# Moving K and score-operand transposes to the DMA crossbar in a chunk-select attention with a gated MLP

## The chip, the cores and the metric

The kernel runs on one core of a Trainium2 chip. The metric is the time of one execution in microseconds (us), the median of several. The kernel before takes 208.53 us (208.47 to 208.6, three runs). The profile's span, from the first to the last instruction, is 206.9 us, about 1.6 us less than the time.

Engines: PE is the matmul engine (PEld its weight loads), ACT is ScalarE, DVE is VectorE, POOL is GpSimd, SP is SyncE. In the traces each takes its instructions in the order that the compiler's scheduler chose, and stands if the next one is not ready (PE stood 10.9 us for one operand in the changed kernel). In this kernel POOL issues all loads from memory, and SP issues all transposes that go by DMA and all stores.

## The reference

Four batches, eight heads, 768 positions, head size 64. K is cut into 24 chunks of 32 positions; the extremes of each chunk give an upper bound on its scores, and each query keeps its six best chunks.

```python
k_min = np.min(k_chunks, axis=3);  k_max = np.max(k_chunks, axis=3)
ub = np.sum(np.maximum(q * k_min, q * k_max), axis=-1)          # per query and chunk; later chunks masked
top_chunks = np.argsort(ub, axis=-1)[..., -top_k:]              # top_k = 6
scores = np.where(selected & causal, scale * (q @ k.T), -1e9)
x = softmax(scores) @ v                                         # heads side by side: 768 x 512 per batch
h = np.maximum(x @ w_in, 0);  u, v = split(h)
v_s = w_spatial @ normalise(v) + b_spatial
out = (u * v_s) @ w_out
```

## The kernel before

The 32 heads are handled as 16 pairs, "pair 0" to "pair 15". The MLP of one batch runs on PE between the scores of the next batch's pairs. For each pair: load K and q (POOL), transpose K, take the chunk extremes (DVE), bound, select (DVE), transpose the score operand `a` (q together with the selection), scores (PE), exponential (ACT), zero the upper triangle (POOL), multiply by V (PE), normalise (DVE).

```python
def k_transpose(self):
    if self.i < 16:                                   # always: 6 PE transposes into PSUM
        self.kT = kT = ps_ml.tile([P, S], F16, tag="mlp", name="kTp")
        for t in range(NQT):
            nc.tensor.transpose(kT[:, t * P:(t + 1) * P], self.k[:, t], identity)
    else: ...                                         # crossbar path, not used
def k_max(self):                                      # k_min is the same with min and negate
    nc.vector.tensor_reduce(self.kmm[:, 0, :], self.kT.rearrange("d (c ch) -> d c ch", ch=CHUNK), axis=AX.X, op=Alu.max)
def k_operand(self, hi):                              # score weights from the transposed K
    copy(self.kh[hi][d0:d1], self.kT[d0:d1])
def a_transpose(self, hi):
    if self.i >= 8:                                   # crossbar, issued by SP
        if hi == 0:
            nc.sync.dma_start_transpose(out=self.a.rearrange("d t h s -> d (t h) s"),
                                        in_=self.qs.rearrange("p t c d -> p (t c d)"))
        return
    ...                                               # else 6 PE transposes into PSUM, for each of two halves
def a_copy(self, hi):
    if self.i >= 8: return
    copy = nc.vector.tensor_copy if self.i < 2 and hi == 0 else nc.scalar.copy
    copy(self.a[:, :, hi, :], self.tr...)
def triangle(self, hi):                               # from pair 4 on, by POOL, between its loads
    nc.gpsimd.affine_select(out=blk, in_=blk, compare_op=Alu.is_ge, fill=0.0, ...)
def load_w_spatial(j):                                # six loads of 128 rows of 1536 bytes
    nc.gpsimd.dma_start(out=ws_raw[:, j], in_=moe_w_spatial[j * P:(j + 1) * P, :])
```

The softmax here doesn't subtract the row's maximum and nothing guards it: scores larger than these inputs give would overflow.

Of the kernel before, what the change touches and what calls it, by code (L numbers as in the profile page):

```python
# [11 lines left out]
F16 = mybir.dt.float16  # L12
Alu = mybir.AluOpType
Act = mybir.ActivationFunctionType
AX = mybir.AxisListType

P = 128
CHUNK = 32
# [30 lines left out]
def kernel(  # L49
# [11 lines left out]
    nc = tc.nc  # L61
    B, H, S, D = q.shape
    NCH = S // CHUNK
# [14 lines left out]
    sb = ctx.enter_context(tc.tile_pool(name="sb", bufs=2))  # L78
# [78 lines left out]
    class Pair:  # L157
# [6 lines left out]
            self.e = {}  # L164

        def k_transpose(self):
            if self.i < 16:
                self.kT = kT = ps_ml.tile([P, S], F16, tag="mlp", name="kTp")
                for t in range(NQT):
                    nc.tensor.transpose(kT[:, t * P:(t + 1) * P], self.k[:, t], identity)  # L170
            else:
                self.kT = sb.tile([P, S], F16, tag="kT", name="kT", bufs=3)
                nc.sync.dma_start_transpose(out=self.kT.rearrange("d (t s) -> d t s", s=P),
                                            in_=self.k.rearrange("p t h d -> p (t h d)"))

        def k_max(self):
            self.kmm = sb.tile([P, 2, NCH], F16, tag="kmm", name="kmm")
            nc.vector.tensor_reduce(self.kmm[:, 0, :], self.kT.rearrange("d (c ch) -> d c ch", ch=CHUNK),  # L178
                                    axis=AX.X, op=Alu.max)

        def k_min(self):
            nc.vector.tensor_reduce(self.kmm[:, 1, :], self.kT.rearrange("d (c ch) -> d c ch", ch=CHUNK),  # L182
                                    axis=AX.X, op=Alu.min, negate=True)

        def k_bounds(self):
            for hi, (d0, d1) in enumerate(HALF):
# [54 lines left out]
        def a_transpose(self, hi):  # L241
            if hi == 0:
                self.a = sb.tile([P, NQT, 2, P], F16, tag="a", name="a")
            if self.i >= 8:
                if hi == 0:
                    nc.sync.dma_start_transpose(out=self.a.rearrange("d t h s -> d (t h) s"),
                                                in_=self.qs.rearrange("p t c d -> p (t c d)"))
                return
            self.tr = self.trans_tile()
            for t in range(NQT):  # L250
                nc.tensor.transpose(self.tr[:, t * P:(t + 1) * P], self.qs[:, t, 2 * hi:2 * hi + 2, :], identity)  # L251

        def a_copy(self, hi):
            if self.i >= 8:
                return
            copy = nc.vector.tensor_copy if self.i < 2 and hi == 0 else nc.scalar.copy
            copy(self.a[:, :, hi, :], self.tr.rearrange("d (t s) -> d t s", s=P))  # L257


# [252 lines left out]
    p, n = pairs[0:2]  # L512
# [82 lines left out]
```

## Time and profile before

| | before |
|---|---|
| time | 208.53 us |
| PE, ACT, DVE busy | 91%, 76%, 75% of the span |
| K reduction from PSUM, two per pair | 0.95 us each |
| K operand copy from PSUM, two per pair | 0.55 us each |
| 192 KB K load, issue to landing (median) | 8.1 us |

The page of the kernel before, parts 1 to 6, in part. The rows of digits cut the span into 40 slices of 5.2 us; a digit is the busy share in tenths. PEclk is the clock granted to PE. The q1 line is the queue of transposes and stores: packets, MB, share. The group lines give busy us and mean ns of one; the last lines give KB per issue and median us from issue to landing.

```profile
PE 187.8 (91%) x1922; PEld 115.1 (56%) x1922; DVE 154.5 (75%) x454; ACT 158.1 (76%) x326; POOL 80.5 (39%) x100
...
PE   0368999898899999999999999999999999999992
...
PEclk9999999999999999999999999999999999999999
DMA  5999999999999999979998926648782124540356
...
q1 hardware_dynamic: 37856, 14.75, 36.4%
...
PE 69%; ACT 17%; DVE 8%; issue 2%; DMA 2%; POOL 0%; DVEq 0%; ACTq 0%; POOLq 0%
...
L178 DVE TENSOR_REDUCE kmm<-kTp 128x24 f16<-128x768 f16 x16 | 15.2, 948 | 3.7 <-PE kTp L170 2.7
...
L194 DVE COPY kh<-kTp 64x768 f16<-64x768 f16 x30 | 16.5, 549 | 0.5
...
k<-in_k_dram POOLq DMA_DIRECT2D x14, 192.0 KB, 8.1
qs<-in_q_dram POOLq DMA_DIRECT2D x14, 192.0 KB, 7.5
ws_raw<-in_moe_w_spatial_dram POOLq DMA_DIRECT2D x6, 192.0 KB, 6.9
```

From the 12th slice (57 us) on PE stands at 9, and from 90 to 152 us it is busy throughout. The chain of waits is two thirds PE (69% of the span), so PE's work is what counts there. In the first 80 us the DMA row stands at 9: nearly all loads fall into this stretch, and a load there mostly takes 6 to 9 us to land. POOL issues the loads and also makes the triangles, in one order. In the timeline of the kernel before, pair 4's first triangle stands behind eight or so loads:

```profile
49.62 0.55 POOL L363 DMA_DIRECT2D w_out_sb<-in_moe_w_out_dram  x1 [1.14 <-DMA vt<-in_v_dram]
50.84 2.04 POOL L327 DMA_DIRECT2D k<-in_k_dram  x2 [0.67 <-PE sc L266]
52.93 0.86 POOL L278 TENSOR_SCALAR_AFFINE_SELECT e<-e 128x768 f16<-128x768 f16 x1
```

The columns are start, duration, instruction, and in brackets how long POOL stood and for what. POOL already waits 1.14 us for an earlier load to land before it can issue another one.

### The profile page before, as it was taken

The page shows a single profiled execution, that of the slowest core. Times are in us where ns is not written, and L with a number is a line of the kernel's source. Part 1 is how long each engine was busy: PE and PEld are TensorE (multiplying, and loading weights), DVE is VectorE, ACT ScalarE, POOL GpSimd, SP SyncE. Part 2 cuts the span into 40 slices and gives each one's busy share as a digit, 9 for nine tenths or more (in the row PEclk, how much of TensorE's full clock was granted, in tenths as well). Part 3 has the DMA queues.
Part 4 walks back from the last instruction along what each step waited for, and adds up shares of the span by engine and source line. Part 5 has one row for each costly group of instructions (what it writes and reads, how often), then busy time and mean ns, then how long its engine had stood idle before and what let it go on. Part 6 is the DMA issues. An engine that isn't in the chain of part 4 may idle for free.

```text
span 206.9 us, 5068 instructions
## 1 busy us (share of the span) xinstructions
PE 187.8 (91%) x1922; PEld 115.1 (56%) x1922; DVE 154.5 (75%) x454; ACT 158.1 (76%) x326; POOL 80.5 (39%) x100
## 2 busy tenths in 40 slices
PE   0368999898899999999999999999999999999992
PEld 0266776775666665656655656565555454444440
DVE  6467979989799989899797999887647456365520
ACT  4797989899998889785989996669999830666042
POOL 7997659596992463236114111111111110000000
PEclk9999999999999999999999999999999999999999
DMA  5999999999999999979998926648782124540356
GB/s 38 92 118 154 140 178 158 173 177 167 177 162 162 97 119 128 135 130 147 149 278 153 180 62 57 127 88 158 181 166 65 38 29 92 187 152 3 72 128 256
DMA packets 114424, 27.27 MB, mean 132 GB/s; under 512 B 109536, under 2 KB 110816, under 8 KB 114400
## 3 DMA queue, kind: packets, MB, share of 16 engines
q0 software_dynamic: 76544, 12.20, 89.8%
q1 hardware_dynamic: 37856, 14.75, 36.4%
q8 instruction: 15, 0.25, 0.5%
q14 instruction: 9, 0.07, 0.1%
HBM read 24.38 MB, written 6.29 MB: 148 GB/s over the span
## 4 chain that ended last, share of the span: by engine, by line
PE 69%; ACT 17%; DVE 8%; issue 2%; DMA 2%; POOL 0%; DVEq 0%; ACTq 0%; POOLq 0%
PE mlp L388 40%; PE sc L266 12%; ACT e L271 10%; PE acc L289 7%; PE kTp L170 2%; ACT a L257 2%; DVE kmm L178 2%; PE ub L222 2%; DMA k<-in_k_dram 2%; PE trm L251 2%; ACT vraw L398 1%; PE tr L205 1%; DVE vn L412 1%; DVE kmm L182 1%; ACT u L420 1%
## 5 line engine op out<-in xcount | busy, mean ns | idle before, releaser
L271 ACT ACTIVATE e<-sc 128x512 f16<-128x512 f32 x192 | 96.9, 553 | 14.8 <-PE sc L266 13.4
L266 PE MATMUL sc<-a,kh 128*128 128x512 f16 (+3 forms) x256 | 65.5, 308 | 2.1 <-ACT e L271 1.5
L388 PE MATMUL mlp<-w_in_sb,xT 128*128 128x512 f16 x192 | 53.0, 379 | 0.1
L278 POOL TENSOR_SCALAR_AFFINE_SELECT e<-e 128x768 f16<-128x768 f16 x24 | 20.9, 869 | 66.3 <-ACT e L271 66.3
L289 PEld LDWEIGHTS <-e 128*128 128x128 f16 x672 | 31.4, 97 | 17.0 <-DVE x L297 3.8
L388 PE MATMUL mlp<-vn,wsT 128*128 128x512 f16 x144 | 37.3, 379 | 0.0
L289 PE MATMUL acc<-vt,e 128*128 128x65 f16 x672 | 35.3, 193 | 0.7 <-DVE x L297 0.4
L266 PEld LDWEIGHTS <-kh 128*128 128x128 f16 x256 | 22.7, 98 | 13.3 <-issue 0.8
L437 ACT COPY o<-mlp 128x512 f32<-128x512 f32 x24 | 14.1, 586 | 19.5 <-PE mlp L388 19.1
L400 DVE BATCH_NORM_STATS2 stats<-vraw 128x6 f32<-128x512 f32 x24 | 16.6, 693 | 12.9 <-ACT vraw L398 12.5
L388 PE MATMUL mlp<-w_out_sb,gT 128*128 128x512 f16 x96 | 25.1, 379 | 0.0
L388 PEld LDWEIGHTS <-xT 128*128 128x128 f16 x192 | 17.2, 97 | 12.6 <-issue 0.4
L427 DVE SCALAR_TENSOR_TENSOR g<-mlp,b_col,u 128x512 f16<-128x512 f32 x24 | 17.9, 748 | 7.3 <-PE mlp L388 6.2
L232 DVE MAX8 max<-ub 128x8 f32<-128x8 f32 (+4 forms) x160 | 15.6, 165 | 5.1 <-PE ub L222 4.9
L388 PEld LDWEIGHTS <-wsT 128*128 128x128 f16 x144 | 12.9, 98 | 10.4
L178 DVE TENSOR_REDUCE kmm<-kTp 128x24 f16<-128x768 f16 x16 | 15.2, 948 | 3.7 <-PE kTp L170 2.7
L297 DVE TENSOR_TENSOR x<-acc,rec 128x384 f16<-128x384 f32 x32 | 17.6, 551 | 0.4
L336 POOL DMA_DIRECT2D qs<-in_q_dram x14 | 14.6, 1049 | 5.9 <-PE sc L266 5.9
L194 DVE COPY kh<-kTp 64x768 f16<-64x768 f16 x30 | 16.5, 549 | 0.5
L398 ACT ACTIVATE vraw<-mlp 128x512 f32<-128x512 f32 x24 | 14.4, 601 | 3.0 <-PE mlp L388 3.0
L420 ACT ACTIVATE u<-mlp 128x512 f16<-128x512 f32 x24 | 14.3, 598 | 1.7 <-PE mlp L388 1.5
L327 POOL DMA_DIRECT2D k<-in_k_dram x14 | 14.4, 1045 | 2.5 <-PE kTp L170 1.8
(67 smaller groups left out, 230.2 us busy)
## 6 DMA issues: line engine op xcount, KB each, us to landing
out_dram<-o SPq DMA_DIRECT2D x24, 256.0 KB, 2.3
vt<-in_v_dram POOLq DMA_DIRECT2D x8, 384.0 KB, 8.8
k<-in_k_dram POOLq DMA_DIRECT2D x14, 192.0 KB, 8.1
qs<-in_q_dram POOLq DMA_DIRECT2D x14, 192.0 KB, 7.5
ws_raw<-in_moe_w_spatial_dram POOLq DMA_DIRECT2D x6, 192.0 KB, 6.9
w_in_sb<-in_moe_w_in_dram POOLq DMA_DIRECT2D x8, 128.0 KB, 6.9
w_out_sb<-in_moe_w_out_dram POOLq DMA_DIRECT2D x4, 128.0 KB, 7.9
k<-in_k_dram POOLq DMA_DIRECT2D x4, 96.0 KB, 3.4
```

Source lines behind the costliest of these rows:

```text
L178: nc.vector.tensor_reduce(self.kmm[:, 0, :], self.kT.rearrange("d (c ch) -> d c ch", ch=CHUNK), axis=AX.X, op=Alu.max)
L194: copy(self.kh[hi][d0:d1], self.kT[d0:d1])
L266: mm(sc[:, col:col + n], lhsT=self.kh[hi][:, t * P:(t + 1) * P], rhs=self.a[:, q0 // P:(q0 + n) // P, hi, :], start=True, stop=not diag)
L271: nc.scalar.activation(out=self.e[hi][:, g * 512:g * 512 + width], in_=sc[:, 0:width], func=Act.Exp, scale=scale)
L278: nc.gpsimd.affine_select(out=blk, in_=blk, compare_op=Alu.is_ge, fill=0.0, base=0, channel_multiplier=-1, pattern=[[0, NQT], [1, P]])
L289: mm(self.av[:, qi, :], lhsT=self.e[hi][:, c:c + P], rhs=self.v[hi][:, t, 0:D + 1], start=first and n == 0, stop=last and n == len(blocks) ...
L297: nc.vector.tensor_tensor(self.x16[:, :, hi, :], in0=self.av[:, :, 0:D], in1=rec.to_broadcast([P, NQT, D]), op=Alu.mult)
L388: mm(st[group][:, 0:cols], lhsT=lhsT, rhs=rhs, start=(j == 0), stop=(j == n - 1))
L398: nc.scalar.activation(st["vraw"][:, ti, :], h, func=Act.Relu)
L400: nc.vector.bn_stats(stats, st["vraw"][:, ti, :])
L420: nc.scalar.activation(st["u"][:, ti, :], h, func=Act.Relu)
L427: nc.vector.scalar_tensor_tensor(g, in0=vs, scalar=b_col[:, ti:ti + 1], in1=st["u"][:, ti, :], op0=Alu.add, op1=Alu.mult)
```

## The change

The intent is to take transposes from PE, which is full (91% busy), and copies from ACT; to shorten the reductions on DVE by two halvings of the K that now lies in SBUF (that this would be shorter was the author's estimate, which no trace of this case showed); and to give two early copies to DVE.

```diff
         def k_transpose(self):
-            if self.i < 16:
+            if self.i < 6:
                 ... PE transposes
             else:                       # crossbar, issued by SP
+        def k_bound(self, m, op):       # used by k_max and k_min
+            src = self.kT.rearrange("d (c ch) -> d c ch", ch=CHUNK)
+            if self.i >= 6:
+                for n in (16, 8):
+                    half = sb.tile([P, NCH, n], F16, tag=f"half{n}", name=f"half{n}")
+                    nc.vector.tensor_tensor(half, in0=src[:, :, 0:n], in1=src[:, :, n:2 * n], op=op)
+                    src = half
+            nc.vector.tensor_reduce(self.kmm[:, m, :], src, axis=AX.X, op=op, negate=(m == 1))
         def a_transpose(self, hi):
-            if self.i >= 8:
+            if self.i >= 6:             # crossbar
         def a_copy(self, hi):
-            if self.i >= 8:
+            if self.i >= 6:
                 return
-            copy = nc.vector.tensor_copy if self.i < 2 and hi == 0 else nc.scalar.copy
+            copy = nc.vector.tensor_copy if self.i < 4 and hi == 0 else nc.scalar.copy
```

More of the change, by code (lines that the diff above doesn't have):

```diff
@@ L177, in k_max @@
             self.kmm = sb.tile([P, 2, NCH], F16, tag="kmm", name="kmm")
-            nc.vector.tensor_reduce(self.kmm[:, 0, :], self.kT.rearrange("d (c ch) -> d c ch", ch=CHUNK),
-                                    axis=AX.X, op=Alu.max)
+            self.k_bound(0, Alu.max)
+        def k_bound(self, m, op):
[6 more added lines that the diff above has]
+            nc.vector.tensor_reduce(self.kmm[:, m, :], src, axis=AX.X, op=op, negate=(m == 1))
         def k_min(self):
-            nc.vector.tensor_reduce(self.kmm[:, 1, :], self.kT.rearrange("d (c ch) -> d c ch", ch=CHUNK),
-                                    axis=AX.X, op=Alu.min, negate=True)
+            self.k_bound(1, Alu.min)
         def k_bounds(self):
```

## The prediction

> **What bounds the kernel now.** The page gives PE 91%, ACT 76%, DVE 75% of 206.9 us. In the table of stretches PE is busy throughout from 90 to 152 us, and the chain of waits there is almost only MLP matmuls, two per 0.43 us: PE-bound. From 20 to 75 us the chain runs through ACT (exponentials, score-operand copies L257) and DVE (28.9 to 36.5 us): from 30 to 45 us PE is busy 13.6, DVE 14.4, ACT 14.0 us. The page's DMA row stays at 9 up to about 78 us: the loads' queue is saturated, and a 192 KB load takes 8 us to land.
>
> **What changes, costed.**
> - PE loses 84 transposes (60 of K, 24 of score operands). Six take 0.35 us in the chain, so 4.9 us, 3.2 us of it after pair 6's first score (66 us).
> - ACT loses six copies of 0.80 us (pairs 6, 7: between 59.6 and 74.6 us; pairs 2, 3: early). DVE takes two at 0.55 us.
> - DVE: a reduction from PSUM takes 0.95 us. [...] DVE rarely limits there: worth little.
> - DMA gains ten K and two score-operand transposes, about 2.7 MB in 256-byte packets, several in the saturated stretch.
>
> **The catch: order on SP.** In the instruction order of the changed kernel, SP issues the K transposes of pairs 6 to 10 first and only then pair 6's score operand. Pair 10's K transpose waits for its K load, whose second half POOL issues behind pair 4's first triangle (52.9 us). In the trace what is issued at 53.7 us lands at 62.8; with the new traffic I expect 63 to 66 us. So pair 6's operand is issued at 64 to 68 us, though it is selected at 58.7. A transpose under this load took 8.8 us to land (issued 60.9, first packet 65.0), 6.9 and 8.4 us. [...] It lands at 70 to 76 us, while PE, in order, wants it at about 66. PE and ACT then stand 4 to 9 us. From pair 6's start to the end the old kernel takes 140.5 us; I take off 3.2 us of PE and about 0.7 us of ACT relief. A start at 72 us gives a span of about 208.6, and time is 1.6 us more.
>
> **Prediction: 210.5 us**, 8 in 10 between 205.5 and 214.5. Faster by over 2%: 0.17; within 2%: 0.53; slower by over 2%: 0.30.
>
> **What would show it.** PE idle before the first score matmul of pair 6, ended by the DMA of its operand, 4 us or more; pair 10's K transpose issued after 62 us, right before it. [...] PE-bound pairs 0.35 us shorter.
>
> **What would make it wrong.** The K load of pair 10 landing early, or transposes landing within 5 us: 204 us. DMA contention also delaying spatial weights or the operands of pairs 7 to 9: more than 214 us.

The sum reads: pair 6 starts at 72 us, and 140.5 us from there to the end, less 3.2 us of PE and 0.7 us of ACT, make a span of 208.6 us; 1.6 us more is a time of 210.2 us, put as 210.5. The saving on DVE, "worth little", is not in it.

## The result, and the profile after

The changed kernel took 229.87 us (229.12 to 231.76, four runs), against 208.56 us for the kernel before on the same chip. The ratio is 1.103, with a 95% interval from 1.098 to 1.108: 10% slower. Ratios here are the mean time of one kernel's fast runs over that of the other's of the same rounds, so not quite the ratio of the medians that are quoted.

The same lines of the page of the changed kernel, whose slices are 5.7 us:

```profile
PE 187.8 (83%) x1838; PEld 111.5 (49%) x1838; DVE 152.9 (67%) x496; ACT 155.3 (68%) x320; POOL 80.9 (36%) x100
...
PE   0478998865397029999999799999999999999993
...
PEclk9999999999589857999999999999999999999999
DMA  6999999999999993998999999656759042551247
...
q1 hardware_dynamic: 48992, 17.51, 43.5%
...
PE 45%; DMA 28%; DVE 13%; ACT 8%; issue 3%; POOL 2%; DVEq 0%; ACTq 0%; POOLq 0%; SPq 0%
...
k<-in_k_dram POOLq DMA_DIRECT2D x14, 192.0 KB, 10.5
qs<-in_q_dram POOLq DMA_DIRECT2D x14, 192.0 KB, 8.5
ws_raw<-in_moe_w_spatial_dram POOLq DMA_DIRECT2D x6, 192.0 KB, 11.4
```

Three things are to be seen. PE has two holes (it is idle from 54.5 to 60.6 and from 72.7 to 83.6 us), and the granted clock falls at each (to 0.50 from 58 to 64 us and from 79 to 88 us). The chain of waits is 28% DMA where it was 2%. And a weight load takes 11.4 us to land instead of 6.9.

The DVE groups that the change made, from the view of groups with shapes kept apart (columns as in the group lines above):

```profile
L201 DVE COPY kh<-kT 64x768 f16<-64x768 f16 x20 | 10.3, 516 | 0.3
L185 DVE TENSOR_TENSOR half<-kT 128x384 f16<-128x384 f16 x20 | 7.7, 396 | 3.8 <-DMA kT<-k 3.8
L187 DVE TENSOR_REDUCE kmm<-half 128x24 f16<-128x192 f16 x20 | 6.7, 340 | 0.1
L185 DVE TENSOR_TENSOR half<-half 128x192 f16<-128x192 f16 x20 | 4.8, 242 | 0.0
```

The three steps of one extreme take 0.396 + 0.242 + 0.340 = 0.98 us, no less than the 0.95 us of the one reduction before, and a K operand copy 0.52 us instead of 0.55.

Where the time went is read from the start of each pair's first exponential in the two traces:

| point | before, us | after, us | later by |
|---|---|---|---|
| pair 4, last exponential ends | 54.2 | 61.5 | 7.3 |
| pair 6 starts | 66.6 | 84.3 | 17.7 |
| pair 7 starts | 77.8 | 97.6 | 19.8 |
| pair 10 starts | 107.1 | 128.3 | 21.2 |
| pair 15 starts | 158.2 | 179.1 | 20.9 |
| end of the span | 206.9 | 227.6 | 20.7 |

So the whole loss is there by pair 10, in two large steps, and after it almost nothing is won back. The largest waits of the changed kernel between 44 and 62 us, from the view of waits (engine and line, what ended the wait, us in total, times, longest):

```profile
ACT e L278 <- PE sc L273: 7.2, 2, 5.6
PEld L296 <- POOL e L285: 6.2, 1, 6.2
PE acc L296 <- POOL e L285: 6.1, 1, 6.1
```

The same view between 62 and 90 us:

```profile
ACT e L278 <- PE sc L273: 13.4, 5, 11.0
PEld L273 <- DMA a<-qs: 11.4, 1, 11.4
PE sc L273 <- DMA a<-qs: 10.9, 1, 10.9
```

The first stall: PE stands 6.1 us for POOL's triangle of pair 4. POOL's timeline of the changed kernel shows why:

```profile
52.78 0.56 POOL L367 DMA_DIRECT2D ws_raw<-in_moe_w_spatial_dram  x1 [1.81 <-DMA ws_raw<-in_moe_w_spatial_dram]
55.93 0.54 POOL L370 DMA_DIRECT2D w_out_sb<-in_moe_w_out_dram  x1 [2.60 <-DMA vt<-in_v_dram]
56.99 1.02 POOL L334 DMA_DIRECT2D k<-in_k_dram  x1 [0.52 <-DMA k<-in_k_dram]
58.19 1.42 POOL L350 DMA_DIRECT2D vt<-in_v_dram  x1 [0.18 <-issue]
59.67 0.86 POOL L285 TENSOR_SCALAR_AFFINE_SELECT e<-e 128x768 f16<-128x768 f16 x1
```

The triangle comes at 59.67 us instead of 52.93. Before three of these four loads POOL stands for an earlier load to land, and the earlier loads are late. The second stall is the one that the prediction named, the operand of pair 6. What leads to it, in the timelines of POOL and SP of the changed kernel:

```profile
60.49 1.02 POOL L334 DMA_DIRECT2D k<-in_k_dram  x1
71.90 1.21 SPq L173 DMA_TRANSPOSE kT<-k  x1
73.29 4.31 SPq L253 DMA_TRANSPOSE a<-qs  x1
```

The second half of pair 10's K load is issued behind the late triangle, at 60.49, and lands at 71.76. Pair 10's K transpose waits for it and is issued at 71.90, and only then, at 73.29, the transpose of pair 6's operand, which lands 10.3 us later, at 83.60. The operand was ready for it earlier, but not as early as before: this is its selection on DVE, in the kernel before and in the changed one.

```profile
58.33 0.39 DVE L237 TENSOR_TENSOR qs<-ub,max 128x240 f16<-128x240 f32 x1
66.77 0.39 DVE L244 TENSOR_TENSOR qs<-ub,max 128x240 f16<-128x240 f32 x1
```

So of the 17.7 us at pair 6, the first 8.4 are a later selection, after the first stall (in it DVE waited 5.8 us for PE). From the end of the selection to the start of pair 6 it then took 17.1 us (6.1 until SP issued the operand, 10.3 until it landed, 0.7 until the first exponential) where the kernel before took 7.9. The order on SP can account for 6.1 us at most.

### The profile page after: what moved, and what is told of

Read it like the earlier page. It is cut to its first block, busy times and chain, and to the rows that moved or that the text cites. A ratio compares the mean times of both kernels' runs of the same rounds, so it can differ in the third digit from the quotient of the medians.

```text
span 227.6 us, 4968 instructions
## 1 busy us (share of the span) xinstructions
PE 187.8 (83%) x1838; PEld 111.5 (49%) x1838; DVE 152.9 (67%) x496; ACT 155.3 (68%) x320; POOL 80.9 (36%) x100
## 4 chain that ended last, share of the span: by engine, by line
PE 45%; DMA 28%; DVE 13%; ACT 8%; issue 3%; POOL 2%; DVEq 0%; ACTq 0%; POOLq 0%; SPq 0%
PE mlp L395 29%; DMA qs<-in_q_dram 12%; PE sc L273 7%; DMA kT<-k 5%; ACT e L278 5%; PE acc L296 5%; DMA a<-qs 5%; DMA ws_raw<-in_moe_w_spatial_dram 5%; DVE kmm L187 2%; DVE vn L419 2%; DVE x L304 2%; DVE half L185 2%; DMA k<-in_k_dram 1%; DVE max L239 1%; PE trm L258 1%
## 5 line engine op out<-in xcount | busy, mean ns | idle before, releaser
L273 PE MATMUL sc<-a,kh 128*128 128x512 f16 (+3 forms) x256 | 67.6, 314 | 13.6 <-DMA a<-qs 12.3
L395 PE MATMUL mlp<-w_in_sb,xT 128*128 128x512 f16 x192 | 55.2, 389 | 0.5 <-DMA xT<-x 0.5
L285 POOL TENSOR_SCALAR_AFFINE_SELECT e<-e 128x768 f16<-128x768 f16 x24 | 21.1, 878 | 65.5 <-ACT e L278 65.4
L273 PEld LDWEIGHTS <-kh 128*128 128x128 f16 x256 | 23.0, 99 | 26.4 <-DMA a<-qs 13.3
L395 PEld LDWEIGHTS <-xT 128*128 128x128 f16 x192 | 17.7, 100 | 13.5 <-DMA xT<-x 0.9
L350 POOL DMA_DIRECT2D vt<-in_v_dram x8 | 11.5, 1438 | 25.3 <-PE sc L273 23.6
L395 PEld LDWEIGHTS <-wsT 128*128 128x128 f16 x144 | 13.0, 97 | 10.9
L343 POOL DMA_DIRECT2D qs<-in_q_dram x14 | 14.6, 1046 | 1.3 <-DMA ws_raw<-in_moe_w_spatial_dram 1.1
L419 DVE TENSOR_SCALAR vn<-vraw,mv,rstd 128x512 f16<-128x512 f32 x24 | 12.8, 582 | 1.6 <-ACT rstd L417 1.6
## 6 DMA issues: line engine op xcount, KB each, us to landing
ws_raw<-in_moe_w_spatial_dram POOLq DMA_DIRECT2D x6, 192.0 KB, 11.4
w_out_sb<-in_moe_w_out_dram POOLq DMA_DIRECT2D x4, 128.0 KB, 10.3
```

The lines of the kernel that those rows point to most:

```text
L273: mm(sc[:, col:col + n], lhsT=self.kh[hi][:, t * P:(t + 1) * P], rhs=self.a[:, q0 // P:(q0 + n) // P, hi, :], start=True, stop=not diag)
L343: nc.gpsimd.dma_start(out=t.rearrange("p x t d -> p (x t) d"), in_=source(q, b, h, 2))
L395: mm(st[group][:, 0:cols], lhsT=lhsT, rhs=rhs, start=(j == 0), stop=(j == n - 1))
L419: nc.vector.tensor_scalar(st["vn"][:, ti, :], in0=st["vraw"][:, ti, :], scalar1=st["mv"][:, ti, 0:1], scalar2=st["rstd"][:, ti, :], op0=Al ...
```

## The experiments

18 kernels were run, all with correct results. Each was timed against the kernel before on the same chip. Waits quoted in the text are from the view of waits, landing times from the trace's DMA issues. A run counts as slow here when it is over 1.5% above the fastest of the same kernel. Medians are over all runs. Slow were three of the four runs in program order, and one of four each in the second run of the last pairs (219.61 us), in its partner without halvings (215.25) and in the run with the triangle moved (220.41).

### Two spare transposes, nothing else

The first K transposes that SP issues are those of pairs 6 and 7, at 38 and 39 us. Do they cost anything apart from who waits for them?

```diff
+                if self.i in (6, 7):       # into a tile that nobody reads; K still goes through PE
+                    nc.sync.dma_start_transpose(out=spare..., in_=self.k...)
```

> The kernel before, plus two crossbar transposes of the K of pairs 6 and 7 on SP into tiles that nobody reads (as early as in the changed kernel); every other engine keeps its order, instruction for instruction. Theory A (crossbar transposes starve the loads in the saturated stretch): loads issued from 38 to 46 us land after 12 to 14 us instead of 7 to 8, POOL stalls on its loads and reaches pair 4's first triangle some 6 us late, and the time rises by 4 to 7 us, to 212.5 to 215.5. Theory B (only the order on SP costs time, since an operand waits behind a K transpose): nothing waits for these two, so under 1 us, 208 to 209.5.

Measured: 216.91 us, ratio 1.039 (1.035 to 1.043). The orders on PE, DVE, ACT and POOL are those of the kernel before, so two transposes whose result nobody reads cost 8.2 us. The waits show the first stall of the changed kernel again:

```profile
PEld L293 <- POOL e L282: 7.5, 1, 7.5
PE acc L293 <- POOL e L282: 7.3, 1, 7.3
```

The two transposes took 11.5 and 14.0 us to land, and the loads issued from 38 to 46 us took 11 to 15.6 us (6.1 to 8.4 before). That is Theory A, though the time is above its range (212.5 to 215.5). Issuing took long too: in the changed kernel the second of these two transposes, issued 1.4 us behind the first, held SP for 4.2 us, its other K transposes for 1.2 to 1.9 us.

### The same bytes, not transposed

```diff
-                    nc.sync.dma_start_transpose(out=spare..., in_=self.k...)
+                    nc.sync.dma_start(out=spare[:, :, 0:P], in_=...)    # the same 2 x 192 KB in 256-byte pieces
```

> As dummy67, but the two transfers are plain copies of the same bytes in the same number of 256-byte pieces, from SP. If it is the transposing that starves the loads (A1), the loads keep landing in about 8 us and the time stays within 1 us of before. If any transfer of 768 small packets beside the loads does it (A2), the time is that of dummy67, about 213 to 215 us.

Measured: 210.4 us, ratio 1.009 (1.005 to 1.013), outside both ranges but much nearer to A1. So 6.5 of the 8.2 us are not the bytes but the transposing. The table of stretches, for 41 to 46 us, shows what the DMA engines moved. A line has the stretch, the busy us of PE, PEld, DVE, ACT and POOL with counts, the granted clock, the DMA share, and GB/s as its last number. The kernel before:

```profile
41.00:46.00 5.00, 4.68 (x78) 3.80 (x75) 4.47 (x10) 4.93 (x12) 4.66 (x5) 1.00 1.48 180
```

With the plain copies:

```profile
41.00:46.00 5.00, 4.68 (x79) 3.80 (x77) 4.46 (x10) 4.92 (x12) 4.49 (x5) 1.00 1.27 213
```

With the spare transposes:

```profile
41.00:46.00 5.00, 4.68 (x79) 3.80 (x76) 4.47 (x10) 4.92 (x12) 4.42 (x5) 1.00 1.35 97
```

The rate rises from 180 to 213 GB/s with plain copies and falls to 97 with transposes, all traffic counted. In the trace's DMA records from 38 to 52 us, a 1536-byte packet of the weight load lasts 141 ns on average before and beside the copies, and 298 ns beside the transposes, with single packets up to 2.7 us. The 2048-byte packets of the input weight, some of which ran beside the same transposes, did not lengthen (208 ns, 219 before). And a transpose is not slow everywhere: the fastest 192 KB transpose of the changed kernel, at 105.5 us, landed after 2.8 us, where the two spare ones beside the weight loads took 11.5 and 14.0 us and the plain copies 9 to 10 us.

### Spare transposes later

> The kernel before plus two spare crossbar transposes, now of K of pairs 12 and 13, issued at about 71 us instead of 38 us; nothing reads their result and the other engines' orders are unchanged. Theory A, a transpose is costly only in the stretch from 38 to 52 us where the weight loads with their 1536- and 1024-byte packets are in flight and POOL's triangles stand behind them: 208.0 to 209.7 us, no new wait over 1 us in the largest waits. Theory B, a transpose is costly beside any loads in the saturated stretch: 212 to 217 us as with the transposes of pairs 6 and 7.

Measured: 209.88 us, ratio 1.005 (1.003 to 1.007). Two spare transposes at 71 us cost 1.1 us, just above Theory A's range. The stretch is still full of loads, but of loads in 128-byte packets, and their mean packet duration from 72 to 84 us did not rise (48 ns, before 50). The operand of pair 8, issued some 5 us behind them, landed at 88.8 instead of 86.3 us, and PE waited 1.6 us for it, a wait that the kernel before does not have.

That beside loads in 128-byte packets a transpose cost little more than its bytes is seen in the packet counts too. From 63 to 67 us the changed kernel's trace has some 370 to 470 load packets and 340 to 430 transpose packets each us, and 1170 to 1210 load packets alone in the two us after. So the loads had about a third of their rate while a transpose ran, but the bytes of both together (150 GB/s, then 152) stayed the same. In the kernel before there are 519 load packets (60 of 1024 bytes) and 520 of a transpose from 65.5 to 67.25 us. Beside the spatial weight's load, from 41 to 46 us in the changed kernel, it was otherwise: 101 GB/s in all (180 in the kernel before), and single packets of both kinds lasted up to 2.6 or 2.7 us. What makes them last so long is not shown.

### The order on SP

The rival to the theory of slowed loads was that the order on SP is the loss. Here SP was kept in program order.

> The changed kernel with SP's transfers kept in the program's own order, so that pair 6's score operand is issued right after the K transposes of pairs 6 and 7 and not after that of pair 10. PE's order is the same but for four matmuls. Theory B (SP's order is the whole loss): 206 to 210 us. Theory A+B (starved loads cost the 6 us before 61 us and the later delays, the order costs the 11 us before pair 6): the stall before pair 6 shrinks from 11 us to under 3, that of pair 4 stays near 6 us, and the time is 216 to 221 us.

Measured: 244.77 us, 240.12 to 247.13; three of the four runs, the profiled one among them, are slow, so there is no ratio, but even the fast one (240.12) is far above both ranges. Pair 6's operand was issued at 69.9 instead of 73.3 us, directly after its selection, but DVE now stood 18.9 us in seven waits for K transposes. The size is not to be relied on. It gives no support to the idea that SP's order alone made the loss; since it moved other transfers too, it does not measure what that order costs either.

### Only the score operands of pairs 6 and 7

> The changed kernel with all K transposes back on PE (and so whole reductions from PSUM): what is left is the score operands of pairs 6 and 7 by the crossbar and two copies moved to DVE. Both theories: no K transpose stands before an operand, no transpose runs before 58 us, so no large stall: 206 to 210 us. If the operands of pairs 6 and 7 by themselves land late (issued at 59 us, landing after 68 us), pair 6 starts up to 3 us late and it is 209 to 212 us.

Measured: 218.77 us, ratio 1.046 (1.042 to 1.050). Both theories expected at most 212 us: a miss. K stays on PE; the two early DVE copies are in this run too, 0.6 us by the next one. Pair 6's operand (384 KB, twice a K transpose) was issued at 59.6 us, as soon as it was selected and with nothing ahead of it on SP, and landed only at 71.9, 12.3 us later. Pair 6 starts at 72.7 instead of 66.6. The operand transposes without any K transpose are a loss in this stretch: on PE and ACT they took about 0.35 + 0.8 us per half.

### Only the DVE copies

> The kernel before with only the last part of the change: VectorE copies the first score operand half of pairs 2 and 3. Theory A, VectorE and ScalarE share the early stretch evenly and this part is worth nothing by itself: 208.0 to 209.2 us. Theory B, it takes two 0.8 us copies from a ScalarE that is on the chain of waits: 206.5 to 207.9 us.

Measured: 209.4 us, ratio 1.003 (1.001 to 1.004). The last part of the change, with the order that the scheduler chose for it, is a loss of 0.6 us by itself, just above Theory A's range.

### The change without the early operands

> The changed kernel with the score operands of pairs 6 and 7 back on PE and ScalarE; K of the pairs from 6 on still goes by the crossbar. Theory A, two separate losses: the stall in pair 4 behind the slowed loads stays (POOL before PE, 5 to 7 us), the wait of pair 6 for its operand is gone, and pairs 10 and on still wait for K behind late loads: 217 to 224 us. Theory B, nearly all of the loss is pair 6's late operand: 209 to 213 us. Theory C, the losses overlap and one slow stretch of DMA sets all: 227 to 231 us.

Measured: 225.65 us, ratio 1.080 (1.078 to 1.083). This lies just above Theory A's range. Pair 6 no longer waits for its operand, which had cost some 10 us, but only 4.2 us are won. Pair 6 starts at 75.4, still 8.8 us later than in the kernel before. The stall of pair 4 stays (PE behind POOL, 5.2 us), and in pair 10 a new one comes up: DVE waits for K transposes 9.0 us in three waits, the longest 5.8, and PE and ACT stand behind it. The stalls are not a sum. Removing one uncovers another.

### K by the crossbar for the last pairs only

From pair 12 on the loads are nearly done (the kernel before issues its last one at 110.7 us) and PE is the bound (busy all of the 12 us from 126 to 138 us), so this is where the change should win.

```diff
-            if self.i < 6:
+            if self.i < 12:                                      # halvings from pair 12 on too; a from pair 8, copies as before
+                with tc.issue_after(pairs[self.i - 2].issued.ins):   # K transpose behind the operand of pair i-2
                     nc.sync.dma_start_transpose(kT...)
```

> The kernel before with the crossbar K path and the halvings for pairs 12 to 15 alone, each K transpose issued behind the operand transpose of the pair two earlier. The profile of before has PE as the bound there, and 24 PE transposes at about 0.058 us would be saved, 1.4 us. Theory A, PE's time is what counts there and the crossbar has room: 206.3 to 207.7 us. Theory B, the later K bounds or slower loads of the late pairs eat the gain: 208.2 to 211 us.

Measured: 217.06 us, ratio 1.040 (1.038 to 1.041), outside both ranges, a clear miss. Pair 12's K transpose was issued at 103.3 and landed at 107.5 us; DVE had come to the first halving about 4 us earlier and stood for it, up to 4.4 us in one wait, and DVE's next work (the selection of pair 11, the normalising of pair 9) stood behind it. So the next run issued the transposes earlier, behind the operand of pair i-4.

> K of pairs 12 to 15 by the crossbar as in the run that took 217.06 us, but each K transpose is issued behind the operand transpose of the pair four earlier instead of two, so that it should land at about 88, 93, 107 and 116 us, before VectorE comes to the halvings of that pair (105 us and later in the kernel before). Theory A, the 8.3 us were VectorE standing in order behind a K transpose that had not landed: 206.5 to 209.5 us, no wait of the halvings on a transpose over 1 us. Theory B, halvings or transposes cost by themselves in this stretch: 212 to 218 us.

Measured: 217.41 us, ratio 1.035 (1.031 to 1.040), inside Theory B's range, but its trace shows a wait and not a cost of the halvings by themselves. The scheduler, seeing the transposes earlier, also moved the halvings forward: the first one of pair 12 came to its turn before pair 10's reductions and stood until the transpose landed at 86.8 us. In the view of waits:

```profile
DVE half L186 <- DMA kT<-k: 5.3, 2, 3.0
```

The next run is this one with a place given to the halvings in DVE's order, near where the reductions stood before.

```diff
+                    with tc.issue_after(pairs[self.i - 2].selected.ins):
                         nc.vector.tensor_tensor(half, ...)
```

> Pairs 12 to 15 by the crossbar again, K transposes behind the operand transpose of the pair four earlier, and now also the halvings put behind the selection of the pair two earlier in VectorE's order, near the place of the reductions in the kernel before, so that the K transposes have landed for several us when VectorE comes to them. Theory A, the loss of 8.7 us was the halvings' early place in VectorE's order, where they stand for a transpose: 207 to 210 us and no wait of a halving on a transpose. Theory B, the added transposes cost by themselves here: 212 us or more.

Measured: 210.59 us, ratio 1.007 (1.004 to 1.009). This is 0.6 us above Theory A's range. No wait of a halving on a transpose is left, and 6.8 us are gone by the medians, 5.9 by the ratios. This is the direct test: most of the loss here came from DVE standing in order for a transpose that had not landed. What remains is 1.6 us over the kernel before. PE was spared 24 transposes, 1.4 us, and the kernel still did not become faster.

### Without the halvings

> The same as the run before, with one reduction of the transposed K from SBUF in place of the two halvings and a reduction. In the changed kernel the three steps took 0.34, 0.24 and 0.34 us, together no less than the 0.95 us of the reduction from PSUM. If a reduction from SBUF takes about 0.85 to 0.95 us, halving gains nothing and this run is within 1 us of its partner; if it takes 0.7 us or less, halving was a loss by itself.

Measured: 212.07 us, ratio 1.014 (1.010 to 1.017), 5.3 us better than its partner with halvings (4.5 by the ratios). One reduction from SBUF takes 0.936 us, nearly what it took from PSUM (0.947). The three steps took 0.347 + 0.241 + 0.340 = 0.93 us there. So halving wins nothing on DVE, and the expectation "within 1 us of its partner" failed, it seems because the order changed too: the reductions stand in DVE's order where transposes have landed (one wait of 0.6 us). (The 0.34 us that the expectation gives for the first step is not the changed kernel's; there it took 0.396.)

> The changed kernel with the halvings undone: one reduction of the transposed K from SBUF for each extreme. A reduction from SBUF took 0.936 us in pairs 12 to 15, against 0.98 for the three steps in the changed kernel. Theory A, the stalls come from the transposes alone: 228 to 232 us. Theory B, the halvings add loss by their early place in VectorE's order, as in pairs 12 to 15, where leaving them out took 5.3 us off: 221 to 227 us.

Measured, the same in the changed kernel: 228.37 us, ratio 1.092 (1.089 to 1.095), 1.5 us off 229.87, so Theory A. Ten pairs of halvings are not what makes the large stalls.

### Are wide packets the partner of the transposes?

The weight rows come in packets of 1536 bytes, the K, q and V loads in packets of 128 bytes. The rows of the spatial weight, and in the first pair of runs those of the input weight too, were loaded in 256-byte pieces into padded tiles.

```diff
-    ws_raw = cp.tile([P, NQT, S], F16)
+    ws_raw = cp.tile([P, NQT, NQT, P + 8], F16)
-        nc.gpsimd.dma_start(out=ws_raw[:, j], in_=moe_w_spatial[j * P:(j + 1) * P, :])
+        nc.gpsimd.dma_start(out=ws_raw[:, j, :, 0:P], in_=moe_w_spatial[...].rearrange("p (c e) -> p c e", e=P))
```

> A control for the next run: the kernel before with the rows of two weights (1536 and 2048 bytes) loaded in 256-byte pieces into padded tiles; nothing goes by a new transpose. The bytes are the same, the order of a few instructions moves. 207.5 to 212 us; its own time matters only as the base of the next run.

> The run before this one plus the two spare crossbar transposes of K of pairs 6 and 7 at about 38 us, which cost 8.2 us where the weights came in wide packets. Theory A, transposes and wide packets stall each other: with 256-byte packets [...] the two transposes cost 0 to 3.5 us over the control. Theory B, any loads suffer so when transposes run in this full stretch: 6 to 10 us over the control, and fewer than 600 packets per us in the stretch.

Measured: the control 211.92 us (ratio 1.015, 1.011 to 1.020), with the two spare transposes 210.71 us (1.009, 1.008 to 1.011). The spare transposes cost nothing. But in both kernels POOL's triangle had moved ahead of several loads and POOL stood idle 5 us, so slow loads had time. The next pair changes the spatial weight only.

> Control: the kernel before with only the rows of the spatial weight, 1536 bytes, in 256-byte pieces. POOL's first triangle stays behind more loads than in the first control, nearly as in the kernel before. 208 to 212 us.

> That control plus the two spare crossbar transposes of K of pairs 6 and 7. Theory A, what the transposes disturb are the wide packets: 0 to 3 us over the control. Theory B, the transposes slow loads of any packet size, and it costs time wherever POOL's triangle stands behind the loads: 5 to 9 us over the control, with POOL's triangle the largest wait of PE; then the first pair of runs was free only because its triangle stood ahead of the loads.

Measured: the control 208.72 us (0.999, 0.996 to 1.001), as fast as the kernel before; with the spare transposes 208.92 us (1.000, 0.995 to 1.005). So they cost 0.2 us here and 8.2 us beside the wide packets. The loads still became slower, though: those issued from 42 to 45 us land after 11.6 to 12.3 us against 8.6 to 9.4 in the control, about 3 us more. Beside wide packets the loads of that place took 14.6 to 15.6 us against 7.4 to 8.4 in the kernel before, 7 us more. And the triangle of pair 4 stood ahead of four loads behind which it stands in the kernel before. So two things differ, and one more run keeps the wide packets and moves the triangle alone.

> The kernel before plus the two spare crossbar transposes of K of pairs 6 and 7 at 38 us, with the weight rows in wide packets as they were, but with pair 4's first triangle placed ahead of four loads (the sixth piece of the spatial weight, the first piece of the output weight and two K loads) in POOL's order, as it stood in the control with narrow packets. The other engines' orders are those of the run that took 216.9 us. Theory A, wide packets are what makes the transposes costly: still 4 to 8 us over the kernel before, with PE waiting for POOL's triangle. Theory B, the slowed loads cost time only through the triangle standing behind them: 208 to 210.5 us, although the loads issued from 38 to 46 us still land after 11 to 15 us.

Measured: 217.15 us, ratio 1.039 (1.036 to 1.042). PE no longer waits for the triangle, but the loss is the same. It has moved to the transposes of the spatial weight, which wait for the sixth piece:

```profile
PE wtr L372 <- DMA ws_raw<-in_moe_w_spatial_dram: 6.4, 2, 6.2
```

Moving the triangle does not cure it. The test is not clean, since the sixth piece was also issued later than in the narrow run (57.8 against 51.0 us, behind a second triangle). That narrow packets remove the cost is shown; whether the width of the packets, and not the order on POOL that came with it, does all of it is not isolated. Two things in the kept traces even speak against width as such. The 2048-byte packets of the input weight did not lengthen beside the transposes, as said. And the narrow pieces of the spatial weight stall too, only for a shorter time: with the spare transposes the rate falls from 42 to 44 us to 57 GB/s (182 in the control), and 51 of the weight's 256-byte packets last over 0.5 us; from 44 to 46 us it is back at 186. With the 1536-byte packets it is 60 and then 107. So it is the load of the spatial weight that suffers beside the transposes, and cutting its rows shortens the stall; why is open.

### The change with narrow packets

> The changed kernel with the rows of the spatial weight loaded in 256-byte pieces, as in the control that cost nothing by itself and in which the two spare transposes cost 0.2 us. Theory A, the stall of pair 4 (6 us, PE behind POOL's triangle behind slowed loads) goes away and the later stalls, pair 6's operand and the K transposes behind late loads, stay: 220 to 225 us. Theory B, the later stalls set the time and absorb the gain: 227 to 231 us.

Measured: 220.86 us, ratio 1.060 (1.054 to 1.066), 9.0 us less than the changed kernel. Pair 4 now ends at 54.1 us, as before the change: the first stall is gone from there. Pair 6 starts at 72.0 (before: 66.6) and pair 7 at 88.8 (77.8), both behind their operands; pair 6's was issued at 60.1 and took 11.3 us, pair 7's 12.0. In this kernel the scheduler also put pair 6's operand ahead of pair 10's K transpose, so part of the 9.0 us may be the order on SP. The two are not separated. No version that was run beats the kernel before; the best with any new transpose that is used was 210.59 us.

## Why the prediction was wrong

The prediction was 210.5 us with a range to 214.5; the kernel took 229.87.

- **"PE-bound" from 90 to 152 us, ACT and DVE before that, and loads saturated to 78 us:** this reading of the kernel before held.
- **"Pair 10's K transpose ... first and only then pair 6's score operand":** right. PE stood 10.9 us for the operand of pair 6, with that K transpose issued just before it. The order was right and the sizes were not.
- **The step that failed first: "with the new traffic I expect 63 to 66 us"** for the K load of pair 10. It landed at 71.76. The prediction took its issue from the old trace, 53.7 us, just behind pair 4's triangle, and so gave it 9.3 to 12.3 us to land. It took 11.3, inside that; but it was issued only at 60.49, since the triangle came at 59.67 instead of 52.93. What failed is that the old time of POOL's triangle, and of the loads that POOL waits for before it, was kept. The prediction counted the new traffic by its bytes, as a little more load on a full row. The runs showed that transposes beside the spatial weight's loads are worth far more than their bytes: two of them, unread, cost 8.2 us, and the same bytes as plain copies 1.7 us.
- **A stall that was not in the prediction at all:** pair 4, 6.1 us of PE, before pair 6 is reached. The prediction followed the transposes to those who read them (DVE, PE) and to SP, but not to POOL, whose triangle stands in one order with the loads that the transposes slow. Under "what would make it wrong" it named delayed spatial weights, which is close, but it gave this no time.
- **"Though it is selected at 58.7":** pair 6's operand was selected at 67.2 us, after the first stall. So the catch of the prediction, the order on SP, held the operand for 6.1 us and not for the 14.6 from 58.7 to 73.29.
- **"Lands at 70 to 76 us", from transposes of 7 to 9 us:** it took 10.3 us and landed at 83.6. In the run with the operands alone it took 12.3 us with nothing ahead of it on SP.
- **"From pair 6's start to the end ... I take off 3.2 us of PE and about 0.7 us of ACT relief":** the stretch took 143.3 us instead of 140.3, so 3 us longer and not 3.9 shorter. These 3 us arise before pair 10 (17.7 us late at pair 6, 21.2 at pair 10), behind the second hole; their cause is not settled. DVE's waits for K transposes are 3.8 us in the whole changed kernel, 2.0 of them before pair 6. In the last-pairs runs such waits were worth more: moving the halvings took some 6 us off there.
- **The saving on DVE, an estimate:** the three steps took 0.396 + 0.242 + 0.340 = 0.98 us in the changed kernel, against 0.95 for the reduction that they replaced, and the K operand copy 0.52 instead of 0.55. The saving did not exist: 2 x 0.98 + 2 x 0.52 = 3.0 us per pair now, 2 x 0.95 + 2 x 0.55 = 3.0 us before. The prediction had called it worth little, so the effect on the total is small, but the reason to do that part of the change is gone.
- **The clock was left out.** The granted clock is 0.63 from 60 to 66 us, behind a hole in which PE was busy 0.02 of 6.1 us. Behind the second, where PE was busy 0.02 of 10.9 us, it is 0.50 from 84 to 88 us, and 0.96 from 88 to 92 (table of stretches). Pair 6 to pair 7 took 13.3 us instead of 11.2. That the clock made this difference is argued, not shown.

Not settled: what makes the spatial weight's load and the transposes disturb each other, how much of the operand's 10.3 us is owed to the loads beside it, and what the 1.6 us left in the last-pairs run are.

## What to carry to other kernels

Before giving a transpose to the DMA crossbar, look at what else the DMA engines are doing at that time: in a stretch full of loads a crossbar transpose here took 7 to 14 us to land and slowed the loads beside it, most of all one weight with rows of 1536 bytes (beside two transposes its packets lasted 298 ns on average instead of 141), so work that cost PE 0.35 us came back as stalls of 6 to 11 us. Follow the slowed loads to every engine that waits in order behind them, the engine that issues them first of all. And when an operand changes from an engine's result to a DMA's, give its reader a later place in its engine's order: the scheduler here placed it as if the transpose were quick.
